# Half-row loads of w1 and w2, matmuls on a constant in TensorE's gaps, and a planned order with slack, in a fused gated-attention and multiplicative-FFN kernel

## The chip, the cores and the metric

The kernel runs on one core of one Trainium2 chip. Its time is the device time of a run in microseconds (us), taken over ten runs. TensorE (PE) multiplies matrices into PSUM; VectorE (DVE), ScalarE (ACT) and GpSimd (POOL) do the elementwise work; SyncE (SP) issues every DMA transfer, in order. Each engine executes its own list of instructions in order and waits for the others on semaphores.

## The reference

Two layers are computed. The first is a linear attention with a forget gate, for 4 batches, 8 heads, 768 steps and a head dimension of 48:

```python
f = 1.0 / (1.0 + np.exp(-f_logit))
for t in range(S):
    state = f[:, :, t, :, None] * state + np.einsum('bhd,bhe->bhde', k[:, :, t], v[:, :, t])
    y[:, :, t] = np.einsum('bhd,bhde->bhe', q[:, :, t], state)
```

Its output, laid out as 3072 tokens by 384, is x of the second layer, `((x @ w1) * (x @ w2)) @ w3 @ w_out`, with w1 and w2 of 384 x 1024, w3 of 1024 x 1024 and w_out of 1024 x 384. The weights arrive as 64-bit floats, q, k, v and f_logit as 32-bit floats. The output has 3072 x 384 values of 32 bits.

## The kernel before, in words

**Attention.** The 3072 tokens are cut into 24 units of 128 steps (u = 0 to 23; six units make a batch, and the state passes from one to the next). For a unit, ScalarE makes the gates (`gates`, L321). VectorE scans their products forward (`forward`, L329) and backward (`backward`, L351) and scales q and k with them (Q at L345, K at L359). TensorE multiplies K and Q in pairs of heads (`pairs`, L370, tile pa). ScalarE copies the result (A, L379) and GpSimd zeroes its upper triangle (`causal`, L385, called the select below). TensorE turns K (`turn`, L396, tile pk), forms the values (`value`, L420, and L428 or L435 for what comes from the state) and the state's update (`update`, L456). VectorE makes the new state S from it (`state`, L466 to L472), ScalarE puts S into blocks (`blocks`, L478). The output ys (L485) is brought into the FFN's layout xt: for units 0 to 3 by a matmul (`moved`, L509, called the move) and a copy (L514), later by ten small DMA transfers (L504).

**FFN.** Four units make a block of 512 tokens, and there are six blocks. In block 0 the up products, x with w1 (a) and x with w2 (b), are plain groups of three matmuls (`three`, L530). The groups over columns 0 to 511 of the weights work on 256 tokens at a time, those over columns 512 to 1023 on all 512. A group a is copied by ScalarE (L567), its group b multiplied onto it by VectorE (`times`, L572); each group holds one of the five PSUM banks named f until then. Block 1 is partly done so too; the other up products and all down products use a seven-product scheme (`seven`, `down`), which needs differences of the weights (`sum_up`, L1016, and `sum_down`, L1030). w3 and w_out are first multiplied into one matrix wc, by eight folds of eight matmuls (`fold`, L984).

**Weights.** A 64-bit load lands in a part of a big tile, `place` (the list `raws`), and is converted in pieces of 512, 768 or 1024 columns (`fetch`). For each piece ScalarE does two operations (L916 and L919) and VectorE four (L922, L923, L927, and the join at L933). Before the change each row block of w1 and w2 (128 x 1024) is one load of 1 MB and is converted in two halves, `c0:c1`. There are five places for the first five loads; a later one takes one of three places and waits until the last reader of that place is done. So the sixth load, the third of w2, waits for a conversion.

**What sets the order.** Nothing is written out by hand: every step is a task of a `Plan`, with an engine, a cost in us, the tasks it waits for, and a priority. `Plan.order` goes through planned time: again and again it takes the task that can start earliest, and of several the one with the lowest priority number. A task that waits for one of another engine counts that one's end plus `lag` (0.2 us, more for DMA). The instructions are then emitted in the order of planned starts, each engine's list in that order. `need(u)` gives the priority of unit u's attention, `due` that of a piece of weights; a PE task of the attention has a large negative priority, so it goes ahead of an up group that could start at the same planned time. The plan decides order alone; when an instruction really starts is decided by the semaphores.

v of a unit is loaded into one of three tiles vt, and a fourth load waits for the first one's readers.

Of the kernel before, what the change touches and what calls it, by code (L numbers as in the profile page):

```python
# [45 lines left out]
P = 128  # L46
# [5 lines left out]
DM = H * D  # L52
# [15 lines left out]
HIGH = float.fromhex("0x1.dffffep+16")  # L68
FLOOR = 2.0**-60
# [3 lines left out]
class Plan:  # L73
# [9 lines left out]
    def add(self, eng, cost, emit, deps=(), prio=0.0, takes=(), frees=(), lag=0.2):  # L83

        t = {
            "eng": eng, "cost": cost, "emit": emit, "deps": [d for d in deps if d is not None], "prio": prio,
            "takes": list(takes), "frees": list(frees), "lag": lag, "at": None, "end": None, "no": len(self.tasks),
        }
        self.tasks.append(t)
        return t  # L90

    def order(self):
        free, done, left = {}, [], list(self.tasks)
        enders = {}
        for t in self.tasks:
            for f in t["frees"]:
                enders.setdefault(id(f), []).append(t)

        def start(t):

            waits = list(t["deps"])
            for name in t["takes"]:
                n, taken = self.slots[name]
                if len(taken) >= n:
                    waits += enders[id(taken[-n])]
            if any(d["end"] is None for d in waits):
                return None
            return max(
                [free.get(t["eng"], 0.0)] + [d["end"] + (d["lag"] if d["eng"] != t["eng"] else 0.0) for d in waits]
            )  # L110

        while left:
            at, _, _, t = min(
                ((at, t["prio"], t["no"], t) for t in left if (at := start(t)) is not None), key=lambda x: x[:3]
            )
            t["at"], t["end"] = at, at + t["cost"]
            free[t["eng"]] = t["end"]
            for name in t["takes"]:
                self.slots[name][1].append(t)
            left.remove(t)  # L120
            done.append(t)
        return sorted(done, key=lambda t: (t["at"], t["no"]))
# [51 lines left out]
def ranged(ctx, tc, q, k, f_logit, v, w1, w2, w3, w_out, out, ident, w12, wc, left):  # L174
# [36 lines left out]
    raws = [at(a, 2048).bitcast(U32) for a in (0, 2048, 4096, 8192, 10240)]  # L211
# [19 lines left out]
    coming = plan.add("PE", 0.0, lambda: None, takes=["ab"], prio=-1e9)  # L231

# [47 lines left out]
    def need(u):  # L280
        return (0.0, 1.0, 2.0, 3.0)[u] if u < 4 else 45.0 + 14.5 * (u - 4)
# [4 lines left out]
    def moves(issue, size, rate, emit, deps, prio):  # L286

        i = plan.add("SP", issue, emit, deps, prio, lag=0.6)
        return plan.add("DMA", size / rate, lambda: None, [i], prio, lag=1.3)

    def attention(u):
        s, t = st[u], tk[u]
        opens, closes = u % NCH == 0, u % NCH == NCH - 1
        n0 = need(u)

# [8 lines left out]
        def free(n, *names):  # L304

            if u < 4:
                return []
            return asked[4:5] + [tk[u - n if u - n >= 4 else u % n][nm] for nm in names]
# [5 lines left out]
        def load_v():  # L314
            s["v"] = loads.tile([P, DM], F32, name="vt")
            nc.sync.dma_start(s["v"], v[u])

        t["lv"] = moves(0.45, 197, 320, load_v, past(u, 3, "v", "s"), n0 - 27)
# [56 lines left out]
        t["a"] = plan.add("PE", 1.1, pairs, [t["q"], t["k"]] + past(u, 1, "y" if u > NPE else "m"), n0 - 1000)  # L375
# [16 lines left out]
        if not closes:  # L392
# [7 lines left out]
            t["t"] = plan.add("PE", 0.45, turn, [t["k"]] + past(u, 1, "d"), n0 - 999)  # L400
# [40 lines left out]
        def y_block(b):  # L441
# [4 lines left out]
            n0 - 998, takes=["f"] if u < NPE else [],  # L446
        )

        if not closes:
# [11 lines left out]
            t["s"] = plan.add("PE", 0.6, update, [t["e"], t["lv"]] + past(u, 1, "d"), n0 - 997)  # L461
# [408 lines left out]

    def fetch(loads_, a, prio, subs, deps=()):
# [18 lines left out]
        buf = load_no if load_no < len(raws) else (load_no - len(raws)) % NRAW  # L890
        raw = raws[buf][:, 0 : 2 * total]
        words = raw.rearrange("p (n two) -> p n two", two=2)
        held = [g for no, b_, gs in users if b_ == buf for g in gs]
# [5 lines left out]
        ld = moves(0.45, total, 380, load, held[-2:], prio)  # L899
        asked.append(ld)  # L900
        got = []
        users.append((load_no, buf, got))
# [46 lines left out]

    def weights():  # L950
        due = {(0, 0): 5.0, (1, 0): 8.0, (0, 1): 24.0, (1, 1): 26.0}
        pieces.update({key: [] for key in due})
        for which, w in enumerate((w1, w2)):
            for kc in range(KM):

                loads_ = [(slice(0, P), w[kc * P : kc * P + P].unsqueeze(1))]
                ends = fetch(loads_, 1, (-26.0, -16.5)[which] + 0.1 * kc, [
                    (
                        half * 512, half * 512 + 512,
                        lambda which=which, kc=kc, half=half: w12[:, which, kc, half * 512 : half * 512 + 512],  # L960
                        due[which, half] + 0.1 * kc, [],
                    ) for half in range(2)
                ])
                for half in range(2):
                    pieces[which, half].append(ends[half])

        def held(buf):
            return [g for _, b, gs in users if b == buf for g in gs]

        done = []  # L970
        for i in range(0, KF, 2):
# [3 lines left out]
                held(4) + [tk[3]["q"]],  # L975
# [24 lines left out]
        for jc in range(KF):  # L1000
            src = w3[jc].unsqueeze(1)
            got = fetch([(slice(0, P), src)], 1, 36 + 6 * jc, [(
                0, KF * P, w3_piece(jc), 56 + 6 * jc, fp[jc - 2 : jc - 1] if jc >= 2 else held(3),
# [49 lines left out]
    for u in range(NU):  # L1053
# [5 lines left out]
        if u % UB == UB - 1:  # L1059
            ffn(u // UB)  # L1060
    for t in plan.order():
        t["emit"]()
# [338 lines left out]
```

## Time and profile before

| what | value |
|---|---|
| median of 10 runs | 508.3 us (507.65 to 508.86) |
| the profiled execution's own time | 508.06 us |
| its span, first to last instruction | 505.7 us |
| TensorE busy | 487.0 us, 96% of the span |
| VectorE busy | 362.7 us, 72% |
| ScalarE busy | 161.8 us, 32% |
| GpSimd busy | 42.3 us, 8% |
| DMA | 46.02 MB, mean 91 GB/s |

The profile is of one execution. Busy time is the time in which an engine works on an instruction; the idle time before an instruction is put down to what released it last. A name such as `f<-xt,w` is written tile and read tiles; `128x256` is partitions by elements. A matmul of 32-bit floats has two records in the trace, so a group of three matmuls is six. "Granted clock" is the TensorE clock that the throttle granted, as a share of full speed. The profile shows the first instructions near 0.3 us; TensorE's first matmul starts at 8.6.

### The profile page before, as it was taken

Reading aid. Unit: us, or ns where it says so; the run is one execution under the profiler, and the core shown is the slowest. Engines: PE = TensorE matmul, PEld = TensorE weight load, DVE = VectorE, ACT = ScalarE, POOL = GpSimd, SP = SyncE. Lnnn points to the kernel's source line nnn. Section 1 sums busy time; section 2 is a strip of 40 time slices with the busy share of each in tenths; the row PEclk is TensorE's granted clock in tenths of the full one; section 3 lists DMA queues with packets and bytes.
Section 4 is the critical chain, followed back from the end, with each engine's and each line's share of the span. In section 5 each row is a group of like instructions: output and inputs, shape, how many; then the busy total and the mean of one; then the engine's idle time right before and its main releaser. Section 6 shows DMA issues by size and latency. Waiting matters only on the chain.

```text
span 505.7 us, 8806 instructions
## 1 busy us (share of the span) xinstructions
PE 487.0 (96%) x3346; PEld 407.0 (80%) x3346; DVE 362.7 (72%) x701; ACT 161.8 (32%) x340; POOL 42.3 (8%) x51
## 2 busy tenths in 40 slices
PE   3889999999999999999999999999999999999995
PEld 2778854666698887889888899888899888889994
DVE  6899999999988769866677766256564677564541
ACT  4689464863434345222332112321010011011000
POOL 8120010010001201001110000110000000000000
PEclk9999999999999999999999999999999999999999
DMA  6968466763223265311160001210002100000011
GB/s 173 373 230 280 131 226 216 253 196 82 54 80 94 59 192 160 95 36 46 45 191 17 1 6 32 59 49 0 2 21 61 45 1 0 1 0 1 32 48 53
DMA packets 30163, 46.02 MB, mean 91 GB/s; under 512 B 6560, under 2 KB 20384, under 8 KB 28320
## 3 DMA queue, kind: packets, MB, share of 16 engines
q1 hardware_dynamic: 30112, 45.38, 28.6%
q8 instruction: 28, 0.46, 0.4%
q14 instruction: 23, 0.19, 0.1%
HBM read 36.70 MB, written 4.72 MB: 82 GB/s over the span
## 4 chain that ended last, share of the span: by engine, by line
PE 91%; DVE 4%; POOL 1%; DMA 1%; issue 1%; SPq 0%; POOLq 0%; DVEq 0%
PE f L530 68%; PE f L984 8%; PE pa L370 5%; PE pa L420 4%; PE pk L456 2%; PE pa L435 2%; PE pk L396 2%; DMA vt<-in_v_dram 1%; DVE fwd L329 1%; PE f L420 1%; DMA ab<-in_f_logit_dram 1%; DVE bwd L351 0%; DVE Q L345 0%; SPq L299 0%; DVE K L359 0%
## 5 line engine op out<-in xcount | busy, mean ns | idle before, releaser
L530 PE MATMUL f<-xt,w 128*128 128x256 f32 (+1 forms) x600 | 160.1, 397 | 0.0
L530 PEld LDWEIGHTS f<-xt,w 128*128 128x128 f32 x600 | 112.9, 190 | 24.4 <-issue 9.5
L530 PE MATMUL f<-place 128*128 128x192 f32 (+1 forms) x504 | 114.0, 351 | 0.0
L530 PEld LDWEIGHTS f<-place 128*128 128x128 f32 x504 | 87.3, 190 | 6.8 <-issue 1.1
L385 POOL TENSOR_SCALAR_AFFINE_SELECT A<-A 128x1024 f32<-128x1024 f32 x24 | 30.9, 1287 | 294.0 <-ACT A L379 294.0
L984 PE MATMUL f<-place 128*128 128x384 f32 x128 | 43.1, 490 | 0.0
L633 ACT COPY a<-f 128x256 f32<-128x256 f32 x36 | 13.4, 372 | 75.5 <-PE f L530 59.7
L530 PE MATMUL f<-xt,place 128*128 128x256 f32 x144 | 37.2, 381 | 0.0
L984 PEld LDWEIGHTS f<-place 128*128 128x128 f32 x128 | 23.8, 190 | 15.8 <-issue 0.5
L530 PE MATMUL f<-wc,ab 128*128 128x192 f32 x192 | 35.6, 329 | 0.0
L530 PEld LDWEIGHTS f<-wc,ab 128*128 128x128 f32 x192 | 31.8, 190 | 0.9
L657 DVE TENSOR_TENSOR place<-f,a 128x256 f32<-128x256 f32 x36 | 15.2, 423 | 23.8 <-PE f L530 23.7
L329 DVE TENSOR_TENSOR_SCAN fwd<-gate,floor 112x512 f32<-112x512 f32 x24 | 30.2, 1256 | 2.8 <-ACT gate L321 1.9
L379 ACT COPY A<-pa 128x1024 f32<-128x1024 f32 x24 | 24.2, 1010 | 22.3 <-PE pa L370 22.3
L370 PEld LDWEIGHTS pa<-Q,K 48*128 48x128 f32 x384 | 24.9, 199 | 6.9 <-issue 4.7
L351 DVE TENSOR_TENSOR_SCAN bwd<-gate,back 112x512 f32<-112x512 f32 x24 | 29.8, 1240 | 0.8
L530 PEld LDWEIGHTS f<-xt,place 128*128 128x128 f32 x144 | 26.9, 189 | 3.8 <-DVE place L657 0.2
L370 PE MATMUL pa<-Q,K 48*128 48x128 f32 x384 | 29.7, 297 | 0.0
L485 ACT ACTIVATE ys<-pa 112x512 f32<-112x512 f32 x20 | 11.9, 597 | 41.0 <-PE pa L435 20.6
L396 PE MATMUL pk<-ident,K 112*128 112x112 f32 x80 | 12.4, 280 | 11.7 <-DVE K L359 10.5
L916 ACT ACTIVATE place<-place 128x512 f32<-128x512 f32 (+2 forms) x24 | 21.2, 885 | 6.7 <-DVE w L933 4.4
L919 ACT ACTIVATE place<-place 128x512 f32<-128x512 uint32 (+2 forms) x24 | 21.1, 888 | 7.1 <-DMA place<-in_w_out_dram 4.0
(104 smaller groups left out, 624.4 us busy)
## 6 DMA issues: line engine op xcount, KB each, us to landing
place<-in_w_dram SPq DMA_DIRECT2D x14, 1024.0 KB, 5.3
vt<-in_v_dram SPq DMA_DIRECT2D x24, 192.0 KB, 3.0
out_dram<-o SPq DMA_DIRECT2D x24, 192.0 KB, 2.1
q<-in_q_dram SPq DMA_DIRECT2D x46, 96.0 KB, 2.5
f<-in_f_logit_dram SPq DMA_DIRECT2D x44, 96.0 KB, 2.6
k<-in_k_dram SPq DMA_DIRECT2D x44, 96.0 KB, 2.6
place<-in_w_out_dram SPq DMA_DIRECT2D x4, 768.0 KB, 5.1
xt<-ys SPq DMA_DIRECT2D x120, 24.0 KB, 1.8
```

Source lines behind the costliest of these rows:

```text
L329: nc.vector.tensor_tensor_scan(s["P"], gate[u % 2][:, 0:NQ], floor, 0.0, ALU.mult, ALU.max)
L351: nc.vector.tensor_tensor_scan(s["R"][:, ::-1], gate[u % 2][:, NQ:0:-1], back[:, ::-1], 0.0, ALU.mult, ALU.max)
L370: nc.tensor.matmul(s["pa"][:, par, cols], lhsT=s["K"][rows(par), cols], rhs=s["Q"][rows(par), cols], start=True, stop=True,)
L379: nc.scalar.copy(s["A"].rearrange("p r h c -> p r (h c)"), s["pa"])
L385: nc.gpsimd.affine_select(out=a, in_=a, pattern=[[0, H], [1, C]], compare_op=ALU.is_ge, fill=0.0, base=0, channel_multiplier=-1,)
L396: nc.tensor.transpose(out=s["pk"][:, hp], in_=s["K"][:, hp * C : hp * C + C], identity=ident[0:R, 0:R])
L420: nc.tensor.matmul(y_block(b)[64 * half : 64 * half + w], lhsT=s["v"][:, h * D : h * D + w], rhs=s["A"][:, par, hp], start=bank not in met ...
L530: nc.tensor.matmul(out_, lhsT=lhs[i], rhs=rhs[i], start=start and i == 0, stop=i == len(lhs) - 1, skip_group_check=True,)
L657: nc.vector.tensor_tensor(ups["u3", k], q["Y"], q["a"], ALU.add)
L916: nc.scalar.activation(m, hi.bitcast(F32), AF.Abs)
L919: nc.scalar.activation(lo.bitcast(F32), lo, AF.Copy, bias=2.0, scale=2.0**-51)
L984: nc.tensor.matmul(w3s["p", jc], lhsT=w3s[jc][:, kc * P : kc * P + P], rhs=wos[:, kc], start=(kc == 0), stop=(kc == KF - 1),)
```

## The change

Six things are edited; the line numbers of the changed kernel are some ten to twenty higher.

1. w1 and w2 are loaded by half rows: twelve loads of 0.5 MB (128 x 512), the first halves of w1's three row blocks, then w2's, then the second halves. Ten half places take the first ten; a load now waits for every reader of any part of its place (`holders`). Later loads rotate over the same three places as before.
2. `idle(n)` emits n matmuls of 256 columns on the constant tile `floor` into an f bank that nobody reads. Nine stand first on TensorE. More are put in where the plan leaves TensorE idle before planned time 35 (`FULL`), one for each 0.43 us. In the built program these are five between unit 0's update and unit 1's turn, and two between unit 3's update and unit 3's value.
3. `slack`: the attention's matmuls (`pairs`, `turn`, `value`, `update`) of units 4 and up count every task of another engine as 0.8 us later in the plan. `late` does the same for the transfers of weights: up to 3.5 us for the first three loads, 3.0 for the loads of w_out and w3.
4. v of unit 3 has a place of its own in `place`; units 4 to 6 therefore follow the unit four before them. The v loads of units 0 to 3 have earlier priorities.
5. The priority of attention from unit 4 on begins at 60 instead of 45, and that of w3's pieces at 50 instead of 56.
6. Unit 4 on waits for the ninth weight load instead of the fifth, which is the same share of w1 and w2 but for a half.

In the built order this moves, among others: both last moves (units 2 and 3) ahead of the first up group; the third state ahead of the first weight piece on VectorE; the first product with w2 from tenth to fourth among the up groups; unit 4's pairs from the middle of block 0's up groups to behind the second fold.

```diff
-    def add(self, eng, cost, emit, deps=(), prio=0.0, takes=(), frees=(), lag=0.2):
+    def add(self, eng, cost, emit, deps=(), prio=0.0, takes=(), frees=(), lag=0.2, slack=0.0):
...
-                [free.get(t["eng"], 0.0)] + [d["end"] + (d["lag"] if d["eng"] != t["eng"] else 0.0) for d in waits]
+                [free.get(t["eng"], 0.0)] + [d["end"] + (d["lag"] + t["slack"] if d["eng"] != t["eng"] else 0.0) for d in waits]
...
-    raws = [at(a, 2048).bitcast(U32) for a in (0, 2048, 4096, 8192, 10240)]
+    halves = [a + i for a in (0, 2048, 4096, 8192, 10240) for i in (0, 1024)]
...
+    def idle(n):
+        to = ps_f.tile([P, TB], F32, name="f")[:, 0:TH]
+        for _ in range(n):
+            nc.tensor.matmul(to, lhsT=floor[:, 0:P], rhs=floor[:, 0:TH], start=True, stop=True)
+
+    plan.add("PE", 7.8, lambda: idle(9), prio=-1e8)
...
-        return (0.0, 1.0, 2.0, 3.0)[u] if u < 4 else 45.0 + 14.5 * (u - 4)
+        return (0.0, 1.0, 2.0, 3.0)[u] if u < 4 else 60 + 14.5 * (u - 4)
...
-        return plan.add("DMA", size / rate, lambda: None, [i], prio, lag=1.3)
+        return plan.add("DMA", size / rate, lambda: None, [i], prio, lag=1.3 + late)
...
+        slack = 0.8 if u >= NPE else 0.0
...
-            return asked[4:5] + [tk[u - n if u - n >= 4 else u % n][nm] for nm in names]
+            return asked[8:9] + [tk[u - n if u - n >= 4 else u % n][nm] for nm in names]
...
-            s["v"] = loads.tile([P, DM], F32, name="vt")
+            s["v"] = at(12288 + NQ, DM) if u == 3 else loads.tile([P, DM], F32, name="vt")
...
-        t["lv"] = moves(0.45, 197, 320, load_v, past(u, 3, "v", "s"), n0 - 27)
+        t["lv"] = moves(0.45, 197, 320, load_v, [] if u == 3 else past(u, 4 if u in (4, 5, 6) else 3, "v", "s"), n0 - (28.2, 28.2, 28.2, 29.6, 27)[min(u, NPE)])
...
+    def holders(where, n):
+        return [g for a, m, gs in users if a < where + n and where < a + m for g in gs]
...
-        buf = load_no if load_no < len(raws) else (load_no - len(raws)) % NRAW
-        raw = raws[buf][:, 0 : 2 * total]
+        if load_no < 2 * 2 * KM:
+            where = halves[load_no % len(halves)]
+        else:
+            where = 2048 * ((load_no + 1) % NRAW)
+        raw = at(where, 2 * total).bitcast(U32)
...
-        ld = moves(0.45, total, 380, load, held[-2:], prio)
+        ld = moves(0.45, total, 380, load, held, prio, max(0.0, 3.5 - 1.2 * load_no) if load_no < 4 * KM else 3.0)
...
+        for half in range(2):
+            for which, w in enumerate((w1, w2)):
+                for kc in range(KM):
+                    c0 = half * KH * P
+                    src = w[kc * P : kc * P + P, c0 : c0 + KH * P].unsqueeze(1)
+                    pieces[which, half] += fetch(
+                        [(slice(0, P), src)], 1, -26 + 9.5 * half + 0.5 * which + 0.1 * kc,
+                        [(0, KH * P, w12_part(which, kc, c0), due[which, half] + 0.1 * kc, [])],
+                    )
...
-                0, KF * P, w3_piece(jc), 56 + 6 * jc, fp[jc - 2 : jc - 1] if jc >= 2 else held(3),
+                0, KF * P, w3_piece(jc), 50 + 6 * jc, fp[jc - 2 : jc - 1] if jc >= 2 else holders(8192, 2048),
...
+    ready_at = 0.0
     for t in plan.order():
+        if t["eng"] == "PE" and t["at"] < FULL:
+            n = int((t["at"] - ready_at) / 0.43)
+            if ready_at and n:
+                idle(n)
+            ready_at = t["end"]
         t["emit"]()
```

## The prediction

> **What bounds the kernel now.** I read the busy time by stretch first, because shares of the whole span hide stages. Columns: stretch, its length, then busy time and instruction count of TensorE (PE), its weight loads, VectorE (DVE), ScalarE (ACT), GpSimd (POOL), granted clock, DMA share, GB/s.
>
> ```profile
> 0.00:8.60 8.60, 0.00 (x0) 0.03 (x1) 5.39 (x13) 2.94 (x5) 7.70 (x19) 1.00 0.57 152
> 8.60:20.00 11.40, 9.51 (x89) 8.05 (x90) 8.94 (x14) 5.42 (x12) 4.76 (x10) 1.00 0.89 297
> 20.00:40.00 20.00, 18.70 (x202) 16.32 (x203) 19.35 (x34) 17.21 (x36) 4.01 (x3) 1.00 0.77 278
> 40.00:60.00 20.00, 20.00 (x89) 16.47 (x88) 19.11 (x40) 14.10 (x27) 0.00 (x0) 1.00 0.57 199
> ```
>
> From 40 us on PE has no hole: over the later stretches length less busy time is 0.04 + 0.44 + 0.65 + 0.45 = 1.6 us up to 500. PE is the bound there, and the change takes no matmul away. A gain can come only from the first 40 us, where DVE is nearly full. So I read both engines in order of time there (start, duration, engine, line, operation; in brackets the idle time before it).
>
> ```profile
> 8.60 0.98 PE L396 MATMUL pk<-ident,K 112*128 112x112 f32 x4 [8.60 <-DVE K L359]
> 9.51 2.08 PE L370 MATMUL pa<-Q,K 48*128 48x128 f32 x16
> 11.52 1.09 PE L456 MATMUL pk<-vt,kt 128*64 128x48 f32 x16
> 14.49 0.98 PE L396 MATMUL pk<-ident,K 112*128 112x112 f32 x4 [1.89 <-DVE K L359]
> ...
> 23.84 1.16 PE L370 MATMUL pa<-Q,K 48*128 48x128 f32 x16
> ...
> 33.33 0.60 PE L396 MATMUL pk<-ident,K 112*128 112x112 f32 x4 [1.11 <-DVE S L471]
> ...
> 36.53 1.56 PE L530 MATMUL f<-xt,w 128*128 128x256 f32 x6
> ```
>
> The same pairs (L370) cost 2.08 us at 9.5 and 1.16 at 23.8: PE runs at half speed until about 19.2, though the granted clock reads 1.00. The first up group (L530) starts at 36.53; it follows the last join (L933) of w1's first column halves, which ends at 35.78.
>
> ```profile
> 12.66 0.36 DVE L469 TENSOR_TENSOR S<-pk,G 112x192 f32<-112x192 f32 x1 [0.66 <-PE pk L456]
> 12.93 1.42 DVE L359 TENSOR_TENSOR K<-k,bwd 112x512 f32<-112x512 f32 x1
> ...
> 19.97 0.36 DVE L471 TENSOR_TENSOR S<-pk,S 112x192 f32<-112x192 f32 x1 [1.36 <-PE pk L456]
> 20.36 0.36 DVE L472 TENSOR_TENSOR S<-S,G 112x192 f32<-112x192 f32 x1
> 20.64 1.58 DVE L345 TENSOR_TENSOR Q<-q,fwd 112x512 f32<-112x512 f32 x1
> ...
> 26.72 1.19 DVE L923 TENSOR_SCALAR place<-place 128x512 uint32<-128x512 uint32 x1
> ...
> 35.09 0.69 DVE L933 CUSTOM_DVE_ANT_0 w<-place,w 128x1024 uint16<-128x1024 uint16 x1
> ```
>
> DVE waits twice for slow PE (0.66 and 1.36). Three operations are stretched by 0.7 to 0.9 (K 0.69 elsewhere, Q 0.68, L923 0.43); each time GpSimd's causal select (L385) runs beside it, and a fourth meets L923 at 29.61.
>
> **The change part by part.** Durations are those rows at full PE speed: turn 0.55 (L396), pairs 1.1, update 0.6 (L456), value 1.05 without and 2.1 with state, moved 1.4 (L509), an up group of 256 columns 1.30; one weight piece of 512 columns 2.13 on DVE (35.70 to 37.83).
>
> *Fillers.* Nine matmuls of 256 columns (0.43 each at full speed by the up group's 1.30 for three, 0.87 at half) start when DVE has set the constant, 2.1. All at half speed they end at 9.9, all fast at 6. The first turn can start at 8.60. Here a rule and the trace differ. The Trainium skill, "TensorE: Matmul & The Clock Gate", section Part 1, lets PE pass from half to full clock after about 3.4 us of sustained work, in a free-running window. The trace shows 4.0 us of work (8.60 to 12.61) without a change, then 4.8 us (14.49 to about 19.25) until it comes. By the rule the fillers are fast from 5.5 and end at 7.8 (a window later: 8.9 and 9.3). By the row's 4.8 us they are fast from 6.9 and end near 8.4. Either is soon enough, because DVE cannot use the first update before 11.94; I take 8.6. Five more fillers follow the first update: 2.2 us from 10.85, over at 13.0, before the next turn.
>
> *DVE's chain, step by step.* Start 4.97 and everything up to 11.94 stay. (1) Turn, pairs and update end at 10.85, so the first S starts at 12.0: 0.66 saved. (2) GpSimd's ten copies end at 12.27 in both kernels; the select follows to 13.4, and K of unit 1 ends 0.54 after it, as now: 13.95 instead of 14.35. (3) Turn, value, pairs, update: 13.95 + 0.55 + 1.05 + 1.1 + 0.6 = 17.25, before DVE needs it at 18.05, so the 1.36 goes. The second select still costs 0.75: Q of unit 2 ends at 20.5 instead of 22.22. (4) Scans, K and Q of unit 3, 4.1: 24.6 instead of 26.34. (5) The third S, 0.9, now stands ahead of the weights, and the third select costs 0.75: 26.2. (6) Three pieces of w1, 6.4, and the fourth select 0.76: 33.4, instead of 35.78. (7) Three pieces of w2, 6.4: 39.8.
>
> *PE's chain.* Turn of unit 3 ends at 26.4, value of unit 2 at 28.5, update 29.1. Two fillers stand here and cost 0.87 on PE's own path, for value of unit 3 has its select at 29.1. Then value to 32.1, the two moves to 34.8, both ahead of the first up group now. Three groups with w1: 38.7. The fourth needs w2's three half pieces, at 39.8 plus the hop: 39.85, so PE stands still for 1.1.
>
> *Sum.* Now, PE has one move (1.44) and three groups (3 x 1.30) still to do at 36.53; the same point is reached at 36.53 + 1.44 + 3.90 = 41.87. Changed: 39.85. Gain 2.0 us. The groups behind it are the same work. Bounds: if w2 is in time, 38.7, gain 3.2; if DVE is 2 us later than walked, none.
>
> *Half rows.* Twelve loads of 0.5 MB for six of 1 MB: six more issues on SP, 0.43 each, 2.6 us, with the q, k and f loads of units 4 and 5 behind them. Now the third w2 load is issued only at 40.66, and nine groups with w1 alone stand before the first with w2. Changed, six half loads (3.1 MB) are issued from 14.2; at the measured 297 GB/s they need 10.6 us plus some 3 of landing, 28, and ACT wants the last at 33.7. Hidden. Without that cover each microsecond late goes on the 39.85. The v loads moved ahead push f of units 2 and 3 back by 0.45 each; ACT then makes their gates at about 10.5 and 13.3, and DVE scans them at 14.6 and 20.5 in the walk above. Hidden too; an f late by more than three microseconds would show.
>
> *Weights ahead of attention.* Unit 4's first scan falls back and its pairs go behind the second fold (L984). Can DVE keep up? From 39.8 to the first w3 row: six pieces 12.8, four w_out pieces at 2.92 (65.27 to 68.19) 11.7, w3 3.8, products 2.7 + 1.8, a state 0.85, a scan 1.25: 34.9, so 74.7. PE: 13 groups 16.9 and eight of 512 columns at 2.61, 20.9: 77.6. Margin 2.9. After it, the last difference of wc (L1030) ends at 142.12 now and the first down group starts at 142.79, a margin of 0.67; the new order plans about a microsecond more. Loss between 0 and 1.
>
> *Slack.* 0.8 us more between producers and the attention's matmuls from unit 4 on. It moves instructions and adds none. It can win back at most the 0.44 idle of 250 to 300, and shift new waits in; I take 0.3 for it and 0.3 against it for the line above. The other 1.1 (0.65 and 0.45) belong to the final judgement and the last down group, which keep their places.
>
> The profiled execution took 508.06 with a span of 505.7, so 2.4 lie around the span and stay. 505.7 - 2.0 = 503.7, or 506.1 in all; runs have a median of 508.3, 0.2 higher: I forecast **506.3**.
>
> **The rivals.**
> *Fillers in the way (slower).* If the fillers do not raise the clock, the first turn starts at 9.9 and the update ends near 13.9; five fillers at 0.87 hold PE to 18.2, while K of unit 1 is ready by 15.5. The second turn comes 3.7 later than now, the second S too, and nothing behind it absorbs that: 508.3 + 3 = 511. It decides where the five cost over 0.62 each ((13.95 - 10.85)/5). For it: 4.0 us of work left PE slow. Against: 7.8 us without a hole precede. 0.07.
> *The gain is swallowed (same).* DVE 1 to 2 us later, by longer select collisions or w2 landing late: PE waits at the fourth group or at the downs. DVE's 19.35 of 20 speaks for it: 508.0. 0.17.
> *Attention too late (slower).* Units 4 to 7 now stand 14 to 24 us later on PE; if VectorE cannot deliver K and Q between the w3 rows, the pairs of units 4 to 11 each wait. At 0.4 a unit that is 3.2 against the 2.0 gained: 509.5; slower begins at 0.38 a unit (2.0 + 1.0 over eight). Against: margins of 2.9 above, and DVE at 75 to 79% after 140. 0.06.
> *No stall at w2 (more).* Gain 3.2 and 0.4 of the idle: 504.7. 0.12.
>
> **How the numbers follow.** The likeliest case has 0.58, its own range 505.2 to 507.3. About 1 us (0.2%) is what a measurement of this kernel can tell from no change. Faster: 0.58 + 0.12 = 0.70; same 0.17; slower 0.13. The range goes from 504.6 to 508.9: of the no-stall case it keeps most, of the swallowed case all, and it leaves out the slow ends and a little below.
>
> **What would show it.** Right: matmuls on the constant from 2 us, the first pairs near 1.16 instead of 2.08; no wait of S for PE at 12 and 18; the last join of w1's half near 33.4 and of w2's near 39.8; the first up group near 34.8 and a hole of about 1 before the fourth; first fold near 77.6; PE's idle from 45 on no more than 1.6. Wrong: pairs still at 2 us, weight pieces waiting for DMA, or holes of PE between 130 and 215. The forecast fails if select collisions differ from one per unit, since they decide where DVE stands at 39.8.

## The result, and the profile after

The changed kernel takes 505.64 us (median; 504.89 to 507.51). The kernel before, run beside it, takes 508.17 us (506.94 to 509.18). The ratio is 0.9954, with a 95% interval from 0.9944 to 0.9963, so about 2.3 us are gained. The forecast was 506.3. The profiled execution of the changed kernel took 506.04 us, with a span of 504.3; before it was 508.06 and 505.7. So of the 2.02 us between these two executions 1.4 lie inside the span, and about 0.6 lie outside it, before the first or after the last instruction. This holds for all executions on record: time less span is 1.68 to 1.84 us in 17 of the changed kernel and 2.09 to 2.41 in 72 of the kernel before.

TensorE (PE) of the changed kernel in order of time, from several stretches (start, duration, engine, line, operation; in brackets idle time and what ended it):

```profile
1.66 6.63 PE L240 MATMUL f<-floor 112*128 112x256 f32 x18 [1.66 <-DVE floor L260]
8.48 0.57 PE L408 MATMUL pk<-ident,K 112*128 112x112 f32 x4 [0.19 <-DVE K L371]
9.02 1.16 PE L382 MATMUL pa<-Q,K 48*128 48x128 f32 x16
...
10.70 2.42 PE L240 MATMUL f<-floor 112*128 112x256 f32 x10
13.08 0.58 PE L408 MATMUL pk<-ident,K 112*128 112x112 f32 x4
...
29.42 1.13 PE L240 MATMUL f<-floor 112*128 112x256 f32 x4
...
35.14 11.17 PE L542 MATMUL f<-xt,w 128*128 128x256 f32 x51
...
76.56 5.43 PE L999 MATMUL f<-place 128*128 128x384 f32 x16
```

The constant matmuls (L240; two records each) run at 1.66, 10.70 and 29.42. The first pairs (L382) now cost 1.16 instead of 2.08 and the first two turns 0.57 and 0.58 instead of 0.98. The first up group (L542) starts at 35.14 instead of 36.53, and from there PE runs through without a hole (that row goes on; its length is cut off at 46 us). The first fold (L999) follows at 76.56.

VectorE (DVE) of the same kernel in order of time:

```profile
11.98 0.36 DVE L481 TENSOR_TENSOR S<-pk,G 112x192 f32<-112x192 f32 x1
...
12.86 1.57 DVE L357 TENSOR_TENSOR Q<-q,fwd 112x512 f32<-112x512 f32 x1
...
17.32 1.56 DVE L371 TENSOR_TENSOR K<-ab,bwd 112x512 f32<-112x512 f32 x1
...
32.43 0.69 DVE L952 CUSTOM_DVE_ANT_0 w<-place,w 128x1024 uint16<-128x1024 uint16 x1
...
38.81 0.69 DVE L952 CUSTOM_DVE_ANT_0 w<-place,w 128x1024 uint16<-128x1024 uint16 x1
...
48.59 0.42 DVE L584 TENSOR_TENSOR ab<-f,ab 128x256 f32<-128x256 f32 x1 [2.57 <-ACT ab L579]
...
75.28 1.23 DVE L952 CUSTOM_DVE_ANT_0 place<-place 128x2048 uint16<-128x2048 uint16 x1
```

S no longer waits for PE at 12. The joins (L952) of w1's and w2's half end at 33.12 and 39.50. Then there is a new wait, 2.57 us before 48.59. The join of the first w3 row ends at 76.51.

Busy time by stretch, first of the changed kernel (stretch, its length, then busy time and count of PE, its weight loads, DVE, ScalarE, GpSimd, then granted clock, DMA share, GB/s):

```profile
8.60:20.00 11.40, 10.09 (x118) 8.32 (x119) 10.83 (x16) 6.00 (x13) 6.24 (x11) 1.00 0.82 231
20.00:40.00 20.00, 20.00 (x203) 17.66 (x201) 19.32 (x35) 18.20 (x39) 2.79 (x2) 1.00 0.99 338
...
140.00:215.00 75.00, 73.95 (x723) 62.52 (x722) 62.92 (x121) 31.56 (x75) 9.01 (x7) 1.00 0.41 116
```

And one stretch of the kernel before:

```profile
140.00:215.00 75.00, 74.96 (x703) 63.81 (x702) 61.91 (x120) 30.01 (x72) 9.60 (x7) 1.00 0.39 113
```

From 8.60 to 20 DVE is busy 10.83 us where it was 8.94. That stretch is where time came from. From 140 to 215 PE lacks 1.05 us where it lacked 0.04: there some of it went back.

PE's new holes are these (changed kernel, in order of time, PE):

```profile
190.07 1.09 PE L432 MATMUL pa<-A,vt 128*48 128x128 f32 x16 [0.43 <-POOL A L397]
...
195.26 1.13 PE L542 MATMUL f<-xt,place 128*128 128x256 f32 x4 [0.62 <-DVE place L669]
...
255.40 0.64 PE L468 MATMUL pk<-vt,kt 128*64 128x48 f32 x16 [0.35 <-DMA vt<-in_v_dram]
```

The kernel before has a smaller one (0.34) at the last of these places. With one of 0.27 at 82.26 and the two that were there before (0.65 and 0.45), PE's idle time from 45 us on is 2.77; before it was 1.58. What led to the first of them is seen on ScalarE (ACT) and on SyncE's queue (SPq) of the changed kernel. On ACT:

```profile
187.33 0.63 ACT L333 ACTIVATE gate<-f 112x512 f32<-112x512 f32 x1 [3.98 <-DMA f<-in_f_logit_dram]
187.86 0.99 ACT L391 COPY A<-pa 128x1024 f32<-128x1024 f32 x1
```

On SyncE's queue:

```profile
175.79 6.53 SPq L516 DMA_DIRECT2D xt<-ys  x10
...
184.39 0.89 SPq L311 DMA_DIRECT2D f<-in_f_logit_dram  x2
...
187.70 7.28 SPq L516 DMA_DIRECT2D xt<-ys  x10
```

ACT executes in order. Its gate waits 3.98 us for an f load, and the copy of A (L391), which the select and then PE's value need, stands behind it. Its f loads were issued at 184.39, behind a gather (L516) of ten small transfers that held the queue until 182.32 and two pairs of loads after it. The plan has these f loads at 177.35, so SyncE is 7.0 us late against its plan; PE is 3.5 late there (its turn planned for 175.02 starts at 178.51). The plan counts 6.2 us for a gather; these two took 6.53 and 7.28.

The second hole leads to a gather too. PE's group at 195.26 waits for a product of DVE (L669), and in front of that stands this one, which waits for xt while the gather at 187.70 holds the queue:

```profile
194.44 0.42 DVE L612 TENSOR_TENSOR place<-xt 128x256 f32<-128x256 f32 x1 [1.30 <-DMA xt<-ys]
```

### The profile page after: what moved, and what is told of

Same layout as the page of the kernel before. It is cut to its first block, busy times and chain, and to the rows that moved or that the text cites. A ratio compares the mean times of both kernels' runs of the same rounds, so it can differ in the third digit from the quotient of the medians.

```text
span 504.3 us, 8896 instructions
## 1 busy us (share of the span) xinstructions
PE 492.9 (98%) x3378; PEld 411.2 (82%) x3378; DVE 363.5 (72%) x701; ACT 161.7 (32%) x340; POOL 46.0 (9%) x51
## 4 chain that ended last, share of the span: by engine, by line
PE 91%; DVE 3%; DMA 2%; SPq 1%; issue 1%; ACT 0%; POOL 0%; DVEq 0%; ACTq 0%; POOLq 0%
PE f L542 67%; PE f L999 8%; PE pa L382 4%; PE pa L432 4%; PE pa L447 2%; PE pk L468 2%; PE pk L408 2%; DMA f<-in_f_logit_dram 1%; PE f L521 1%; DVE bwd L363 1%; DVE fwd L341 1%; SPq L516 1%; PE f L440 1%; PE f L432 1%; DMA xt<-ys 1%
## 5 line engine op out<-in xcount | busy, mean ns | idle before, releaser
L542 PE MATMUL f<-xt,w 128*128 128x256 f32 (+1 forms) x600 | 160.3, 397 | 0.0
L542 PEld LDWEIGHTS f<-xt,w 128*128 128x128 f32 x600 | 112.8, 190 | 25.0 <-issue 10.9
L542 PE MATMUL f<-place 128*128 128x192 f32 (+1 forms) x504 | 113.9, 351 | 0.0
L542 PEld LDWEIGHTS f<-place 128*128 128x128 f32 x504 | 87.4, 190 | 6.3 <-issue 0.6
L397 POOL TENSOR_SCALAR_AFFINE_SELECT A<-A 128x1024 f32<-128x1024 f32 x24 | 34.8, 1450 | 296.1 <-ACT A L391 295.9
L999 PE MATMUL f<-place 128*128 128x384 f32 x128 | 43.2, 491 | 0.3 <-issue 0.3
L542 PE MATMUL f<-xt,place 128*128 128x256 f32 x144 | 37.7, 384 | 0.6 <-DVE place L669 0.6
L999 PEld LDWEIGHTS f<-place 128*128 128x128 f32 x128 | 23.7, 190 | 16.9 <-issue 1.0
L542 PE MATMUL f<-wc,ab 128*128 128x192 f32 x192 | 35.3, 327 | 0.0
L391 ACT COPY A<-pa 128x1024 f32<-128x1024 f32 x24 | 24.3, 1012 | 27.6 <-PE pa L382 27.5
L542 PEld LDWEIGHTS f<-wc,ab 128*128 128x128 f32 x192 | 32.0, 190 | 0.7 <-issue 0.2
L669 DVE TENSOR_TENSOR place<-f,a 128x256 f32<-128x256 f32 x36 | 15.2, 423 | 21.5 <-PE f L542 21.3
L542 PEld LDWEIGHTS f<-xt,place 128*128 128x128 f32 x144 | 26.5, 189 | 4.6 <-DVE place L669 0.8
L382 PEld LDWEIGHTS pa<-Q,K 48*128 48x128 f32 x384 | 23.3, 187 | 7.4 <-issue 4.7
L382 PE MATMUL pa<-Q,K 48*128 48x128 f32 x384 | 27.9, 285 | 0.0
L357 DVE TENSOR_TENSOR Q<-q,fwd 112x512 f32<-112x512 f32 x23 | 18.8, 816 | 9.5 <-PE pa L447 9.5
L432 PEld LDWEIGHTS pa<-A,vt 128*48 128x48 f32 x320 | 17.1, 129 | 7.0 <-issue 6.1
```

Of the source, the lines that this page charges most:

```text
L357: nc.vector.tensor_tensor(s["Q"], qu, s["P"], ALU.mult)
L382: nc.tensor.matmul(s["pa"][:, par, cols], lhsT=s["K"][rows(par), cols], rhs=s["Q"][rows(par), cols], start=True, stop=True,)
L391: nc.scalar.copy(s["A"].rearrange("p r h c -> p r (h c)"), s["pa"])
L397: nc.gpsimd.affine_select(out=a, in_=a, pattern=[[0, H], [1, C]], compare_op=ALU.is_ge, fill=0.0, base=0, channel_multiplier=-1,)
L432: nc.tensor.matmul(y_block(b)[64 * half : 64 * half + w], lhsT=s["v"][:, h * D : h * D + w], rhs=s["A"][:, par, hp], start=bank not in met ...
L542: nc.tensor.matmul(out_, lhsT=lhs[i], rhs=rhs[i], start=start and i == 0, stop=i == len(lhs) - 1, skip_group_check=True,)
```

## The experiments

The theories of the expectations are these. *Theory C*: the gain is the clock's; constant matmuls bring TensorE to full speed before DVE needs it, and the edits of the order hardly matter. *Theory O*: the edits of the order carry the gain or keep it. *Theory S*: what is given back later is due to SyncE, which issues later than the plan believes. *Theory D*: once PE starts early, DVE is the next bound, so a still earlier start gives nothing. The kernel before ran beside each group of runs: 507.77 us beside the first four, 508.34 beside the next four, 508.19 beside the last two. Ratios are to these. The constant matmuls, the half rows and the attention's slack were taken out singly; the place for v of unit 3, the priorities and `late` were not.

### The changed kernel without any constant matmul

```diff
-    plan.add("PE", 7.8, lambda: idle(9), prio=-1e8)
+    plan.add("PE", 7.8, lambda: None, prio=-1e8)
...
-            if ready_at and n:
-                idle(n)
```

> The changed kernel with its order of instructions kept and all sixteen matmuls on the constant left out. Theory C (clock: the gain is VectorE's two waits for a slow TensorE): the first pairs are back near 2.0 us, S of unit 0 waits about 0.7 and S of unit 1 about 1.4, the last join of w1's first half moves from 33.1 to 35.1, the first up group from 35.1 to about 36.3 (without the two fillers it is bound by the join alone), and the median comes out near 507.2. Theory O (order: half rows, the moves ahead of the up groups, and slack give the gain, the clock is hidden): the first up group stays near 35 or comes 0.9 earlier, median 505.0 to 505.7.

Measured: 506.71 us (505.47 to 507.85), ratio 0.9979 (0.9965 to 0.9993). PE of this kernel in order of time:

```profile
9.28 2.08 PE L382 MATMUL pa<-Q,K 48*128 48x128 f32 x16
...
37.53 22.71 PE L542 MATMUL f<-xt,w 128*128 128x256 f32 x100
```

DVE of this kernel:

```profile
20.22 0.36 DVE L483 TENSOR_TENSOR S<-pk,S 112x192 f32<-112x192 f32 x1 [1.84 <-PE pk L468]
```

The slow pairs are back, and so are S's waits for PE (0.67, 1.84 and 0.81). The first up group starts 37.53 - 35.14 = 2.39 us later than with the constant matmuls. So the waits behave as theory C has it, and the start comes out even later than the 36.3 that it expected. But the whole run is only 0.0025 of 508, some 1.3 us, above the changed kernel. Started later, PE seems to find its inputs more often ready: its only new hole from 45 us on is one of 0.19 at 191.62. The order alone, without a single constant matmul, is about 1.1 us faster than the kernel before. Half of that is outside the span (time less span has a median of 1.77, and 2.27 in the kernel before beside it), half inside. Theory C is not the whole of it, and the median lies between what theories C and O expected.

### The kernel before with constant matmuls alone

```diff
+    plan.add("PE", 7.8, lambda: idle(9), prio=-1e8)
...
+    ready_at = 0.0
     for t in plan.order():
+        if t["eng"] == "PE" and t["at"] < 35.0:
+            n = int((t["at"] - ready_at) / 0.43)
+            if ready_at and n:
+                idle(n)
+            ready_at = t["end"]
```

> The kernel before with only the matmuls on the constant added (nine first, then one, four and one where its own plan has gaps; whole rows, old priorities, no slack). Theory C: S of units 0 and 1 stop waiting, w1's half is joined near 33.7 instead of 35.78, the first up group starts near 34.6, median 506.0 to 506.4. Theory O: nothing behind 20 us moves by more than 0.3, median 508.0 to 508.4.

Measured: 508.96 us (507.38 to 511.72), ratio 1.003 (1.0013 to 1.0047). It is slower, but not in every execution, as is told below. The profiled run took 507.6. PE of this kernel:

```profile
35.14 1.13 PE L538 MATMUL f<-xt,w 128*128 128x256 f32 x4
...
255.92 0.61 PE L464 MATMUL pk<-vt,kt 128*64 128x48 f32 x15 [1.17 <-DMA vt<-in_v_dram]
```

SyncE's queue of this kernel:

```profile
237.49 7.61 SPq L512 DMA_DIRECT2D xt<-ys  x10
...
245.82 7.37 SPq L512 DMA_DIRECT2D xt<-ys  x10
253.29 0.53 SPq L324 DMA_DIRECT2D vt<-in_v_dram  x1
```

The start gains what it should: the first up group is at 35.14, 1.39 ahead of the kernel before. At the update that waits for this vt, PE would have been at 255.92 - 1.17 = 254.75; in the kernel before the same update starts at 256.48 after 0.34, so without that wait at 256.14. The difference is still 1.39. But SyncE issues this vt load only at 253.29 (253.01 in the kernel before), behind two gathers of ten. So 1.17 - 0.34 = 0.83 of the 1.39 is taken back at this one place: PE got faster and the queue did not. The judgement's matmul behind it stands 0.70 ahead (379.20 against 379.90). This accounts for the profiled run. The others differ in the clock: four executions with a mean granted clock of 0.997 to 1.0 took 507.38 to 507.60, and the eight with 0.990 to 0.994 took 508.80 to 511.72. So in most executions TensorE's clock fell somewhere, and the time of the median goes with that. Where it fell is not seen, for the profile is of one of the four. With the clock kept, the gain is 0.2 to 0.4 us against 507.77. Theory C, which expected 506.0 to 506.4 from these matmuls alone, falls either way.

### The changed kernel with whole rows of w1 and w2

```diff
-            return asked[8:9] + [tk[u - n if u - n >= 4 else u % n][nm] for nm in names]
+            return asked[4:5] + [tk[u - n if u - n >= 4 else u % n][nm] for nm in names]
...
+        raws = (0, 2048, 4096, 8192, 10240)
+        where = raws[load_no if load_no < 5 else (load_no - 5) % NRAW]
...
-        for half in range(2):
-            for which, w in enumerate((w1, w2)):
-                for kc in range(KM):
+        for which, w in enumerate((w1, w2)):
+            for kc in range(KM):
+                loads_ = [(slice(0, P), w[kc * P : kc * P + P].unsqueeze(1))]
...
```

> The changed kernel with w1 and w2 loaded as six whole row blocks again (fillers, slack and priorities kept). The plan then puts eight groups of 256 columns and one of 512 with w1 ahead of the first with w2. Theory C: the start is the same, w1 joined near 33.1, first up group near 35.1, and since groups with w1 cover the late third load of w2, TensorE has no hole: median 505.4 to 506.0, half rows are worth under 0.3. Theory O: w2 late again, TensorE waits at the first group with w2 or at the second halves, median 507 or more.

Measured: 508.57 us (506.72 to 509.37), ratio 1.0014 (1.0 to 1.0027). The gain is gone. The first up group starts at 35.04, as early as in the changed kernel, and up to 180 us PE has no hole. Then come these (PE in order of time, the three largest of five that the kernel before does not have in this size):

```profile
206.98 1.13 PE L542 MATMUL f<-xt,place 128*128 128x256 f32 x4 [1.00 <-DVE place L669]
...
239.95 1.13 PE L542 MATMUL f<-xt,place 128*128 128x256 f32 x4 [0.92 <-DVE place L669]
...
256.83 0.64 PE L468 MATMUL pk<-vt,kt 128*64 128x48 f32 x16 [1.19 <-DMA vt<-in_v_dram]
```

So half rows do not pay at the start, where the loads they split are used. What they pay shows 150 us later. The plan, with other loads to place, comes out with another order, and that is the likely reason; the run shows that loads and order together lose 3 us against the changed kernel. Which of the many moved instructions does it was not separated. Theory O expected a median of 507 or more and has that right, but not the place: it looked for waits at w2.

### The changed kernel without slack

```diff
-        slack = 0.8 if u >= NPE else 0.0
+        slack = 0.0
```

> The changed kernel with slack 0 for the attention's matmuls (fillers, half rows, priorities and late kept). Theory C: the first 75 us are the same; TensorE's holes from 75 to 300, 1.7 us with slack, become 1.0 to 2.5, median 505.3 to 506.5. Theory O: slack pays by itself, holes of 3 or more, median 507 or more.

Measured: 506.64 us (505.41 to 508.26), ratio 0.9979 (0.9965 to 0.9992), so the slack is worth about 1.3 us, give or take 0.9. The start is the same (first up group 35.16). PE:

```profile
170.07 0.60 PE L408 MATMUL pk<-ident,K 112*128 112x112 f32 x4 [1.38 <-DVE K L371]
...
256.60 0.61 PE L468 MATMUL pk<-vt,kt 128*64 128x48 f32 x15 [1.02 <-DMA vt<-in_v_dram]
```

DVE of the same kernel:

```profile
168.40 1.62 DVE L371 TENSOR_TENSOR K<-k,bwd 112x512 f32<-112x512 f32 x1 [1.73 <-DMA k<-in_k_dram]
```

SyncE's queue:

```profile
158.36 7.04 SPq L516 DMA_DIRECT2D xt<-ys  x10
165.49 1.92 SPq L311 DMA_DIRECT2D k<-in_k_dram  x4
```

Read from the bottom: the k loads are issued at 165.49, right behind a gather that held the queue for 7.04 us. DVE waits 1.73 for k, K is stretched to 1.62, and PE, whose turn stands directly in front of an up group, waits 1.38. With slack the plan puts other groups of the FFN in front of such a turn, so PE has work while K is late. A late v load takes another 1.02 at 256.60. The four holes between 75 and 300 sum to 3.04 (the others are 0.27 and 0.37), as theory O expected; its median of 507 is not reached.

### The changed kernel once more, and with SyncE's costs nearer to the measured ones

```diff
-        t["lf"] = moves(0.87, 197, 250, load(fu, f_logit), free(2, "g"), n0 - 30)
+        t["lf"] = moves(0.95, 197, 250, load(fu, f_logit), free(2, "g"), n0 - 30)
...
-            t["z"] = t["x"] = moves(6.2, 197, 300, gather, [t["y"]] + before, n0 - 100)
+            t["z"] = t["x"] = moves(6.9, 197, 300, gather, [t["y"]] + before, n0 - 100)
```

The loads of k and q are changed like that of f. The changed kernel itself was run again in the same group:

> The changed kernel once more, beside the following three on one chip. Theory C alone (the start decides): 0.9950 to 0.9965 of the kernel before. Theory S (the start's 2.8 us are partly given back between 140 and 260, where SyncE's list of transfers is late, and how much differs from run to run): the same mean, and in the profile holes of TensorE of 0.5 to 2.5 between 160 and 260, each behind a transfer.

Measured: 505.38 us (504.52 to 505.93), ratio 0.9946 (0.9929 to 0.9963); in its profile the new holes are 0.19 at 189.24 and 0.25 at 253.93. So the same kernel gives back 0.4 in one execution and 1.7 in another. Theory S expected holes of 0.5 to 2.5 here; this execution, the fastest of the six, stays below that.

> The changed kernel with one thing different: the plan's costs of SyncE's issues as the trace has them, 6.9 instead of 6.2 for the ten transfers of a gather and 0.95 instead of 0.87 for a pair of loads. No instruction is added or taken, only the order differs. Theory S: the waits behind late transfers between 160 and 260 shrink from 1.4 to under 0.6, median 0.8 to 1.3 us under the changed kernel beside it. Theory C alone: the same median within 0.4.

Measured: 505.69 us, ratio 0.9954 (0.9938 to 0.997); five of six runs lie between 505.65 and 505.73. PE's only hole from 45 us on that the kernel before does not have:

```profile
82.16 5.40 PE L999 MATMUL f<-place 128*128 128x384 f32 x16 [0.58 <-ACT wc L1006]
```

The holes between 160 and 260 are gone, as theory S has it, and the runs hardly differ any more. But the time is not better: the last matmul ends at 498.42 in this profile (496.96 + 1.46), at 497.36 in that of the changed kernel in the same group. (That profile is of the fastest of its six executions; the two medians, 505.69 and 505.38, are not told apart.) Theory S is borne out on what makes the holes, and wrong that their removal is a gain of 0.8 to 1.3. What the new order pays in exchange, without a hole on PE, stays open.

### Constant matmuls of 48 rows

```diff
-            nc.tensor.matmul(to, lhsT=floor[:, 0:P], rhs=floor[:, 0:TH], start=True, stop=True)
+            nc.tensor.matmul(to, lhsT=floor[0:D, 0:P], rhs=floor[0:D, 0:TH], start=True, stop=True)
```

> The changed kernel with the matmuls on the constant over 48 rows instead of 112, as the attention's pairs have; as many columns, as many instructions. If the clock follows the time in which TensorE works, all is as with 112 rows: fillers end near 8.3, pairs at 1.16, the same median. If it follows how much of the array works, the nine stay at half speed and end at 9.3 to 9.5, the five take 4.3, the second turn starts near 17 instead of 13.1, and the median is 2 to 4 us over the changed kernel.

Measured: 510.2 us (509.5 to 513.09), ratio 1.0061 (1.0037 to 1.0086). PE:

```profile
1.66 8.04 PE L240 MATMUL f<-floor 48*128 48x256 f32 x18 [1.66 <-DVE floor L260]
...
10.57 2.08 PE L382 MATMUL pa<-Q,K 48*128 48x128 f32 x16
...
13.60 4.63 PE L240 MATMUL f<-floor 48*128 48x256 f32 x10
18.16 1.01 PE L408 MATMUL pk<-ident,K 112*128 112x112 f32 x4
...
40.27 4.91 PE L542 MATMUL f<-xt,w 128*128 128x256 f32 x22
```

The same number of matmuls of the same 256 columns, without a gap from 1.66 on, but on 48 of the 128 rows. PE stays slow: 0.45 us for a record of the nine and 0.46 for one of the five, pairs of 2.08, a second turn of 1.01 at 18.16. Full speed comes only within the pairs at 20.99 (1.52), behind a value, which uses 128 rows. The five matmuls between the units then cost 4.63 us on the path, and the first up group is 5.1 us late. The time is 4.8 us above the changed kernel beside it, where 2 to 4 were expected. This is the slower rival of the prediction, made real.

### Only the first nine

```diff
-            if ready_at and n:
-                idle(n)
```

> The changed kernel with the first nine matmuls on the constant alone; the five and the two in later gaps are left out. Theory C: the gap of 2.4 us after the first update is too short to slow TensorE, the second turn still runs in 0.6; without the two, value of unit 3 and the moves come 0.9 earlier, the first up group at 34.2, a hole of about 0.5 where the fourth group's third matmul waits for w2: 0.4 better at 40 us, median within 0.5 of the changed kernel. If the five are needed, the second turn and pairs are back at 1.0 and 2.0 and the first up group is near 36.

Measured: 507.12 us (505.74 to 508.6), ratio 0.9979 (0.9966 to 0.9992). PE:

```profile
13.96 0.58 PE L408 MATMUL pk<-ident,K 112*128 112x112 f32 x4 [3.06 <-DVE K L371]
14.47 1.84 PE L432 MATMUL f<-A,vt 128*64 128x128 f32 x16
16.24 2.01 PE L382 MATMUL pa<-Q,K 48*128 48x128 f32 x16
```

By stretch:

```profile
8.60:20.00 11.40, 8.34 (x101) 7.23 (x99) 10.01 (x16) 6.02 (x13) 5.30 (x11) 0.85 0.80 230
```

Without the five, PE stands still for 3.06 us. The turn behind that is still fast, and then value and pairs are slow again (1.84 and 2.01 instead of 1.09 and 1.16); the granted clock of the stretch falls to 0.85. So the gap was not too short, as theory C supposed. In all twelve executions the mean granted clock lies between 0.988 and 0.995. The first up group starts at 35.25, as in the changed kernel, but two matmuls fewer stand before it: the run without those two alone, which comes next, has it at 34.23 and a median of 505.82. Against that run the five are worth 1.0 us at the start and 1.3 in the median. The profile has six holes of 0.3 to 0.7 between 40 and 257, 2.7 in all, where the changed kernel has four, 1.7 in all.

### Without the two before the first up group, with and without the new costs

```diff
-            if ready_at and n:
+            if ready_at and n > 2:
```

> The changed kernel without the two constant matmuls between unit 3's update and its value; the nine and the five stay, and the order. The prediction charged these two 0.87 us of TensorE's own path. Theory C (what counts is when TensorE reaches the up groups, and the order has room): value of unit 3 still waits for its select at about 29.1 to 29.4 and starts there, so the first up group starts at 34.0 to 34.6 instead of 35.14, the groups with w1 alone end 0.6 to 1.1 earlier, and then the group that needs w2's third half piece (joined 39.5) waits 0.3 to 0.8: time between 504.9 and 505.4, not measurably different. Theory D (the start is limited by VectorE's weight pieces, and what is won is lost later): first up group no more than 0.3 earlier, time 505.4 to 506.0. If the two keep the clock up (a gap of 1 us puts TensorE back to half speed), value of unit 3 costs 4 us instead of 3 and the time goes to 507.

Measured: 505.82 us (504.5 to 507.59), ratio 0.9953 (0.9939 to 0.9968). PE:

```profile
34.23 4.91 PE L542 MATMUL f<-xt,w 128*128 128x256 f32 x22
39.41 8.90 PE L542 MATMUL f<-xt,w 128*128 128x256 f32 x40 [0.27 <-DVE w L952]
...
76.85 5.43 PE L999 MATMUL f<-place 128*128 128x384 f32 x16 [0.36 <-DVE place L952]
```

The first up group is 0.91 earlier, and by the first fold nothing of it is left: 0.27 is spent waiting for w2's third half piece, 0.36 waiting for the first w3 row, and the fold starts at 76.85 where the changed kernel has 76.56. (Another 0.57 is lost on the way without showing as idle time.) On the time theory D has it right (505.4 to 506.0), on the start it has not: it expected no more than 0.3 earlier there. Both waits are for weights that DVE converts, so PE gains nothing here by starting earlier.

> Both edits: the plan's costs of SyncE's issues nearer to the measured ones (gather 6.9, a pair of loads 0.95), and without the two constant matmuls. Theory C: as the run with the costs alone (median 505.69, spread between runs under 0.5) less 0.3 to 0.9, so 504.8 to 505.4. Theory D: 505.6 to 505.8, same as with the costs alone.

Measured: 505.8 us (505.56 to 506.24), ratio 0.9952 (0.9935 to 0.9968): as theory D has it, the same as with the new costs alone. No version was found that beats the changed kernel.

## Why the prediction was right, and where it was not

| step, as predicted | predicted | measured |
|---|---|---|
| the nine end | 8.4 by the row, 7.8 to 9.3 by the rule | 8.29 |
| first S | 12.0 | 11.98 |
| Q of unit 2 ends | 20.5 | 20.22 |
| w1's half joined | 33.4 | 33.12 |
| first up group | 34.8 | 35.14 |
| w2's half joined | 39.8 | 39.50 |
| hole before the fourth group | 1.1 | none |
| first w3 row joined | 74.7 | 76.51 |
| first fold | 77.6 | 76.56 |
| PE's idle from 45 on | no more than 1.6 | 2.77 |
| time outside the span | 2.4, stays | 1.7 |

**The clock.** The mechanism was right, and the run without constant matmuls shows it: without them the waits return. The nine start at 1.66, not at 2.1, for PE waits only for the second of DVE's settings of the constant (L260). Their 18 records took 6.63 us in the changed kernel, and from 5.91 to 7.27 in eight other profiles with the same nine. A record takes 0.433 at half and 0.217 at full speed (six of an up group take 1.30), so 5.91 is some nine slow records ((5.91 - 3.90) / 0.217 = 9.3) and 7.27 some sixteen (15.5): full speed came between 4.0 and 6.7 us after the first matmul, differently from one execution to the next. The Trainium skill, "TensorE: Matmul & The Clock Gate", section Part 1, speaks of a free-running window of about 3.4 us that must be busy; since a window may have begun just before the work, an estimate from that page is 3.4 to 6.8, and the rows agree. Where the prediction weighed the rule against "4.0 us of work without a change", it compared unlike work: that work was turns, pairs and updates. The run with 48 rows shows that time alone is not what counts, since 8.0 us of the same matmuls on fewer rows, without a gap, changed nothing there.

**DVE's chain.** It came out within 0.3 us up to 39.5, with one select collision per unit, as assumed. Which operation is stretched was not: Q of unit 1 (12.86) and K of unit 2 (17.32) took some 0.88 each, where the walk had put 0.75 on K of unit 1 and on Q of unit 2. The sum is nearly the same.

**The hole that did not come.** The failed step is "The fourth needs w2's three half pieces, at 39.8 plus the hop: 39.85, so PE stands still for 1.1." A group is three matmuls, and each waits for its own piece. Only the third needs the piece that is joined last. The fourth group started at 35.14 + 3 x 1.30 = 39.04, without a hole; its third matmul is due at 39.04 + 2 x 0.43 = 39.9, and the join had ended at 39.50. So PE gained 41.87 - 39.04 = 2.83 instead of 2.0 by that point (of the two last moves only unit 3's stood behind the first up group before; unit 2's ran at 30.61, so one move is the right count), between the forecast and its upper bound of 3.2. The run without the two matmuls shows where that limit really lies: started 0.91 earlier, PE waits 0.27 for this very join.

**The margin of 2.9.** The first w3 row was to be joined at 74.7, 2.9 before PE wants it. It was joined at 76.51, 0.05 before the fold. The walk left out a wait. ACT of the changed kernel:

```profile
47.40 0.90 ACT L938 ACTIVATE place<-place 128x768 f32<-128x768 uint32 x1 [3.77 <-DMA place<-in_w_out_dram]
48.21 0.35 ACT L579 COPY ab<-f 128x256 f32<-128x256 f32 x1
```

ACT waits 3.77 us for a load of w_out, the copy of an up group stands behind that, and DVE's product (48.59) waits 2.57 for it. This cost PE nothing, but used up the margin of DVE. It is one reason why an earlier start gains nothing more: without the two matmuls PE waits 0.36 for this row.

**Slack and half rows.** Here the prediction was wrong in kind, and the total hides it by luck. It took 0.3 for the slack and 0.3 against it, and put half rows down as hidden. Taking the slack away costs 1.3 us, and going back to whole rows 3. Neither changes when PE reaches the up groups (35.16 and 35.04); in both runs the loss shows in later holes. In the profile of the changed kernel 2.83 were gained by 39 us and 2.77 - 1.58 = 1.19 given back in holes, which leaves 1.64; its last matmul ends 1.50 earlier than before (498.82 against 500.32). The "loss between 0 and 1" was looked for at the sums of wc near 142, where there is none. It lies between 180 and 260, and each of the three holes there leads back to a transfer behind SyncE's gathers.

**Time outside the span.** The forecast let 2.4 us around the span stay. They became 1.7. The constant matmuls do not do it: time less span has a median of 2.29 in the kernel before with them and of 1.77 in the changed kernel without them; with whole rows it is 1.99. So it comes with the loads and the order. What it is stays open. The forecast gain of 2.0 came about as 0.8 more at the start, 1.2 lost in holes and 0.6 from outside the span: its nearness is in good part luck.

**Rivals.** "Fillers in the way" needs fillers that leave the clock low: with 48 rows that is what happens. "The gain is swallowed" is what happened to the kernel with whole rows, at other places than supposed, and in part to the kernel before with constant matmuls alone, where the fallen clock of most executions comes on top. "Attention too late" did not occur: no pairs of units 4 to 11 wait on PE. "No stall at w2" came true, without the idle time won back.

**Taken together.** The order without constant matmuls is 1.1 us faster than the kernel before; the constant matmuls without the order win at most 0.4, and lose where the clock falls; both together win about 2.3.

## What to carry to other kernels

Time won at the start of a kernel bound by one engine can be lost again where the other queues have no room to run ahead by as much; so look where transfers are issued, and compare when they could be issued with when the faster engine will want them. When you cost a wait on several producers, go down to the single instruction that waits: a group of three matmuls starts when its first piece is there. Where a planner fixes the order, slack in front of the work behind loads can pay (0.8 us of it was worth about 1.3 here). Measured issue costs took the waits and most of the spread away, but no time. Expect an edit to show its price a hundred microseconds from where it was made. And look at the granted clock of every run, not only of the profiled one, before you explain a median.

## What the runs showed of the hardware that was not expected

TensorE's speed at the start depended on how many rows a matmul uses. 8.04 us of matmuls on 48 rows without a gap left it at half speed, and it was still there at 18.16, after more than 16 us of unbroken work of which 12.67 was such matmuls; on 112 rows the same matmuls had it at full speed after 4.0 to 6.7 us. After an idle stretch of 3.06 us (the run with the nine alone) one turn was still fast, and then TensorE was slow again.

The granted clock of the profile does not always tell: it reads 1.00 between 8.60 and 20 in the run with 48 rows, where the pairs take 2.08 us, and 0.85 in the run with the nine alone. In these runs it showed a clock that fell from full speed, and did not show the half speed of the start.

In the changed kernel each of the first four selects of GpSimd (they start at 12.30, 17.25, 24.96 and 27.54 and take 1.1 to 1.6 us) has one operation of VectorE beside it that takes 0.8 to 0.9 us longer than its like: Q 1.57 and K 1.56 instead of 0.69, a conversion 1.20 instead of 0.43 (at 25.46), another 1.32 instead of 0.42 (at 27.89). Not every operation beside a select is stretched: the one at 25.00 took its usual 0.42.

A gather of ten small transfers holds SyncE's queue for 6.2 to 8.3 us, differing between gathers and between executions: the last but one before the v load near 255 took 6.21 and 6.22 in the two profiles of the changed kernel, the last 6.84 and 7.12.
